# One fused kernel of block-causal attention and two feed-forward layers: the first pair's queries and keys are issued from ScalarE's queue, and a table shifts the order of the later instructions

## The chip, the cores and the metric

The kernel runs on one core of a Trainium2 chip. The metric is the device time of one execution in microseconds, as the median of several runs; lower is better. A profiled execution has a span, which is the time from its first to its last instruction, and a device time of its own, which is a little longer.

Five engines work side by side, each with a fixed sequence of instructions: TensorE (PE for its matmuls, PEld for its weight loads), VectorE (DVE), ScalarE (ACT), GpSimd (POOL) and SyncE (SP, which here only issues DMAs). An engine waits on semaphores for the others and never overtakes within its own sequence.

## What is computed

The reference, cut to what matters:

```python
def _attn_ref(q, k, v):                       # 4 batches, 8 heads, 576 positions, head size 64
    scores = scale * np.matmul(q, k.transpose(0, 1, 3, 2))
    mask = block_i >= block_j                 # blocks of 64 positions
    scores = np.where(mask, scores, -1000000000.0)
    attn = np.exp(scores - np.max(scores, axis=-1, keepdims=True))
    attn = attn / (np.sum(attn, axis=-1, keepdims=True) + 1e-09)
    return np.matmul(attn, v)

x = attn_out.transpose(0, 2, 1, 3).reshape(2304, 512)
h = np.maximum(np.maximum(x @ w1, x @ w2), x @ w3)      # 512 -> 768
x = h @ w_out                                           # 768 -> 512
h = np.maximum(x @ w_in, 0.0)                           # 512 -> 2048
out = h * h @ w_out2                                    # 2048 -> 512
```

The weights arrive as 64-bit floats and are turned into 32-bit ones on the chip.

## The kernel before

**Stages.** Heads are taken in pairs: pairs 0 to 3 are batch 0, pairs 4 to 7 batch 1, and so on to pair 15. `attn_pair` computes a pair in steps of 128 query rows: scores on TensorE (tiles `sc`, `sc_t`), the mask and the row maximum on VectorE (`nm`), the exponential with its row sum on ScalarE (`P`, `sm`), transposes on TensorE (`tp`), copies of these (`ta`, `tb`), and the product with the values (`av`). For batch 0 the queries and keys of a first group of 256 positions go as plain floats straight from a DMA into the scores; `score_operands_f32` issues the three DMAs of a pair into one tile, `zk0` for pair 0 and `zk1` for pair 1, and `zk_early` for pairs 2 and 3. `mlp1` is the first feed-forward layer on a block of tokens (tiles `l`, `run`, `hh`, `hl`, then `ys`); `mlp1(0)` needs only batch 0's first group, so its matmuls stand beside the attention of the rest. It multiplies in two parts: each 32-bit weight chunk is split in a high and a low part (`w1h`, `w1l` for the first matrix, `wo` for the second). `load_w_` brings one chunk of 128x512 weights: one DMA of 512 KB, two activations on ScalarE, two operations on VectorE, one addition on GpSimd, then a copy on ScalarE for the high part and a subtraction on VectorE for the low part. There are 18 chunks of the first matrices and 6 of `wo`. While attention runs, `quad_forms` prepares the weights of the second feed-forward layer and stores them (`wst` to `ws_d`). From about 364 us on TensorE has only `mlp1` and then the second layer (`ph_x`, `ph_z`, `acc_x`, `acc_z`, `acc_y`) to do.

**The order of the work is made by a planner.** All calls go through the class `Plan`. `note` records an operation with its number, its rank and what it depends on, and `issue` then plays the whole list against a small model of durations and semaphore delays: whichever engine can start something earliest takes, of the operations that can start then, the one with the lowest rank, and among these the lowest number. The operations are issued in that order, so that each engine's sequence is fixed when the program is built. Attention has rank 0, `mlp1` rank 1 (so that its matmuls fill what attention leaves), evictions of `mlp1` rank -1, and the preparation of the second layer's weights rank 2. An operation marked for `nc.any` goes to ScalarE or VectorE, whichever comes first in the model. `issue` runs twice: once for everything up to `mlp1(3)` and `quad_forms`, and once for the rest. Because every instruction goes through `call`, the profile gives most of them one line, L190, and they are told apart by their tiles.

**The start.** A table load and an activation of one column make ScalarE ready for the exponential (L374). GpSimd builds a 128x128 identity. TensorE multiplies that identity with itself eight times (tile `idle`, 16 instructions). SyncE issues the first weight chunk (`raw_w`), then the three DMAs of `zk0`, the values of pair 0, a second weight chunk, the three of `zk1`, and so on.

Of the kernel before, what the change touches and what calls it, by code (L numbers as in the profile page):

```python
# [12 lines left out]
F32 = mybir.dt.float32  # L13
# [135 lines left out]


class Op:
    def __init__(self, index, engines, name, args, kw, rank):
        self.index, self.engines, self.name, self.args, self.kw, self.rank = index, engines, name, args, kw, rank
        self.deps, self.after, self.makes = set(), [], []
        self.engine = self.end = None
# [16 lines left out]
class Plan:  # L172
    def __init__(self, tc):
        self.tc, self.ops, self.rank = tc, [], 0
        nc = tc.nc
        self.real = dict(pe=nc.tensor, dve=nc.vector, act=nc.scalar, pool=nc.gpsimd, sp=nc.sync)
        self.free = dict(pe=1450.0, dve=900.0, act=2240.0, pool=1300.0, sp=740.0)
        self.held, self.queue = dict(dve=0.0, pool=0.0), 0.0
        self.tensor, self.vector, self.scalar = [Engine(self, (e,)) for e in ("pe", "dve", "act")]
        self.gpsimd, self.sync, self.any = [Engine(self, e) for e in (("pool",), ("sp",), ("act", "dve"))]  # L180
# [47 lines left out]

    def issue(self):

        ops, free, held, queue = self.ops, self.free, self.held, self.queue
        left = [0 for op in ops]
        users = [[] for _ in ops]
# [18 lines left out]
        for _ in ops:  # L252
            best = None
            for e, w in waiting.items():
                if not w:
                    continue
                other = held["pool" if e == "dve" else "dve"] if e in held else 0.0
                start = {i: max(free[e], at, other if port else 0.0) for i, (at, port) in w.items()}
                t = min(start.values())
                i = min((i for i, s in start.items() if s <= t), key=lambda i: (ops[i].rank, i))  # L260
                if best is None or t < best[0]:
                    best = t, e, i
# [27 lines left out]
class Engine:  # L290
# [3 lines left out]
    def __getattr__(self, name):  # L294
        return lambda *args, **kw: self.plan.note(self.engines, name, args, kw)


HOLD = dict(dve=120, pool=60)
# [63 lines left out]
def fused_kernel(ctx: ExitStack, tc: tile.TileContext, z0, k0, kz0, qk, v, w123, wo1, win2, wo2, out):  # L362
# [8 lines left out]

    warm = const.tile([128, 1], F32, name="warm")
    tc.nc.vector.memset(warm, 0.0)
    tc.nc.scalar.activation(out=warm, in_=warm, func=AF.Exp)  # L374
    make_identity(tc.nc, ident.tile.real)
    dram = Pool(nc, dram)
# [9 lines left out]
    def bank(name, tag):  # L386
        return ps.tile([128, 512], F32, tag=tag, bufs=BANKS[tag], name=name)


    idle = bank("idle", "av")  # L390
# [108 lines left out]
    def score_operands_f32(n, g):  # L499


        if g == 0:
            if n < 2:
                zk = at.tile([128, 3, GA], F32, tag="tb", bufs=2 * CFG["TB"][1], name=f"zk{n}")
            else:
                if not early:
                    early.append(m1.tile([128, 8, 3, GA], F32, tag="wo1", name="zk_early"))
                zk = early[0][:, n]
# [43 lines left out]
    def attn_pair(n, groups=(0, 1)):  # L552
# [27 lines left out]
        def step(i):  # L580
# [13 lines left out]
            for h in range(2):  # L594
                for c, (qp, kp) in enumerate(score[h]):
                    mm(sc[h][:, :N], qp[:, 128 * i - q0:128 * i - q0 + 128], kp[:, :N], start=c == 0,
                       stop=c == len(score[h]) - 1)
                if not share:
                    nc.vector.memset(sc[h][0:64, N - 64:N], MASKED / scale)
                    nc.vector.tensor_reduce(out=nm[:, h:h + 1], in_=sc[h][:, :N], axis=AX.X, op=ALU.max, negate=True)  # L600
# [256 lines left out]
    with nc.behind(marks[CFG["WO"]][0]), nc.ranked(2):  # L857
        for q in range(NQ):
            quad_forms(1, q)
        for q in range(EARLY):  # L860
            quad_forms(0, q)
    nc.issue()
    es_a.close()
# [312 lines left out]
```

## Time and profile before

| what | value |
|---|---|
| median of three runs | 838.93 us (838.79 to 840.89) |
| the profiled execution | 840.18 us |
| its span, first to last instruction | 838.4 us |
| TensorE busy with matmuls | 825.8 us (99%) |
| TensorE idle in the span | 12.6 us |
| VectorE busy, ScalarE busy | 625.0 us (75%), 474.4 us (57%) |

Times below are microseconds from the span's start. An engine's busy share is an average over stages that are bound by different things, so it has to be read stage by stage. A matmul's end is modelled in the profile and matmuls overlap, so a short wait between two of them need not show as idle time.

### The profile page before, as it was taken

The numbers are of one execution on the slowest core, as the hardware profiler recorded it, in microseconds if no ns is written. First come the engines' busy times: TensorE is split into PE (matmuls) and PEld (weight loads), VectorE is DVE, ScalarE is ACT, GpSimd is POOL, SyncE is SP. The second block draws the span as 40 slices with busy tenths as digits, with TensorE's granted clock in tenths as the row PEclk, the third lists the DMA queues.
The fourth block names the chain that finished last, engine by engine and source line by source line (L and its number), as shares of the span: only waits on it lengthen the run. The fifth ranks groups of instructions, "written<-read, shape, count | busy, mean of one in ns | idle before, by whom it ended". The sixth has DMA issues, their size and how long they took to land.

```text
span 838.4 us, 14621 instructions
## 1 busy us (share of the span) xinstructions
PE 825.8 (99%) x5008; PEld 779.2 (93%) x5008; DVE 625.0 (75%) x1347; ACT 474.4 (57%) x1099; POOL 108.0 (13%) x98
## 2 busy tenths in 40 slices
PE   8999999999999999999999999999999999999998
PEld 6678899988999889999999999999999999999998
DVE  7989789888889988817877557987269855478562
ACT  7999678788778767736554224544124552233441
POOL 2343111221122212202221000000000000000000
PEclk9999999999999999999999999999999999999999
DMA  9755455665566656254796867888988889988882
GB/s 326 263 162 171 124 175 182 203 224 183 167 206 206 199 192 201 77 194 150 264 352 228 312 203 248 286 292 271 306 257 255 257 249 288 293 256 254 246 272 85
DMA packets 92203, 190.24 MB, mean 227 GB/s; under 512 B 9697, under 2 KB 18913, under 8 KB 92129
## 3 DMA queue, kind: packets, MB, share of 16 engines
q1 hardware_dynamic: 92128, 189.31, 69.2%
q8 instruction: 40, 0.66, 0.3%
q14 instruction: 35, 0.28, 0.1%
HBM read 150.47 MB, written 38.80 MB: 226 GB/s over the span
## 4 chain that ended last, share of the span: by engine, by line
PE 90%; DVE 5%; ACT 3%; DMA 1%; POOL 1%; issue 1%; POOLq 0%; ACTq 0%; DVEq 0%
PE l L190 33%; PE ph_x L190 12%; PE acc_x L190 12%; PE ph_z L190 9%; PE acc_z L190 6%; PE av L190 4%; PE sc L190 4%; PE tp L190 3%; PE acc_y L190 3%; PE sc_t L190 2%; DVE nm L190 1%; DMA raw_w<-in_wo 1%; PE tp_t L190 1%; DVE w1l L190 1%; ACT P L190 1%
## 5 line engine op out<-in xcount | busy, mean ns | idle before, releaser
L190 PE MATMUL l<-xhl,w1h 128*128 128x432 f32 (+2 forms) x864 | 230.6, 344 | 0.5 <-DVE xhl L190 0.5
L190 PEld LDWEIGHTS l<-xhl,w1h 128*128 128x128 f32 x864 | 154.0, 188 | 7.5 <-DVE xhl L190 1.2
L190 PE MATMUL l<-xhl,w1l 128*128 128x432 f32 (+2 forms) x432 | 149.7, 347 | 0.6 <-DVE run L190 0.5
L190 PEld LDWEIGHTS l<-xhl,w1l 128*128 128x128 f32 x432 | 81.3, 188 | 5.8 <-DVE run L190 1.4
L190 PE MATMUL ph_x<-t,ws 128*128 128x384 f32 x432 | 80.9, 335 | 0.0
L190 PE MATMUL l<-hh,wo 128*128 128x432 f32 (+2 forms) x288 | 77.5, 344 | 1.2 <-DVE wo L190 1.1
L190 PEld LDWEIGHTS ph_x<-t,ws 128*128 128x128 f32 x432 | 75.6, 188 | 0.0
L190 ACT ACTIVATE P<-sc,nm 128x128 f32<-128x128 f32 (+3 forms) x128 | 67.3, 535 | 11.5 <-DVE nm L190 10.0
L190 DVE TENSOR_TENSOR run<-l,run 128x432 f32<-128x432 f32 (+2 forms) x72 | 39.8, 553 | 32.6 <-PE l L190 29.4
L190 POOL TENSOR_TENSOR f_w<-f_w,raw_w 128x512 int32<-128x512 int32 x30 | 41.5, 1384 | 148.2 <-DVE f_w L190 33.4
L190 DVE TENSOR_REDUCE nm<-sc 128x2 f32<-128x256 f32 (+2 forms) x96 | 55.0, 590 | 0.8
L190 PEld LDWEIGHTS l<-hh,wo 128*128 128x128 f32 x288 | 51.9, 188 | 3.7 <-DVE wo L190 1.3
L190 PE MATMUL acc_x<-g_p,ws 128*128 128x384 f32 x288 | 54.0, 335 | 0.0
L190 PE MATMUL ph_z<-b,ws 128*128 128x384 f32 x288 | 53.9, 335 | 0.0
L190 PE MATMUL tp<-ident,P 128*128 128x128 f32 x320 | 49.9, 275 | 1.1 <-ACT rs L190 0.5
L190 PEld LDWEIGHTS acc_x<-g_p,ws 128*128 128x128 f32 x288 | 50.5, 188 | 0.0
L190 PEld LDWEIGHTS ph_z<-b,ws 128*128 128x128 f32 x288 | 50.4, 188 | 0.0
L190 PE MATMUL l<-hl,wo 128*128 128x432 f32 (+2 forms) x144 | 49.2, 342 | 0.0
L190 PEld LDWEIGHTS tp<-ident,P 128*128 128x128 f32 x320 | 38.8, 141 | 8.9 <-ACT P L190 1.3
L190 PE MATMUL av<-tb,v 128*64 128x320 f32 (+1 forms) x256 | 42.9, 410 | 0.0
L190 ACT COPY tb<-tp 128x384 f32<-128x384 f32 (+1 forms) x64 | 32.4, 539 | 13.4 <-PE tp L190 12.9
L190 DVE TENSOR_TENSOR g_p<-c_wo,g_p 128x768 fp32r<-128x768 f32 x24 | 22.9, 956 | 16.8 <-ACT g_p L190 16.8
(188 smaller groups left out, 1746.5 us busy)
## 6 DMA issues: line engine op xcount, KB each, us to landing
ws<-ws_d SPq DMA_DIRECT2D x336, 256.0 KB, 4.0
ws_d<-wst SPq DMA_DIRECT2D x70, 256.0 KB, 4.4
raw<-in_qk SPq DMA_DIRECT2D x24, 576.0 KB, 4.3
ws_d<-wst SPq DMA_DIRECT2D x21, 512.0 KB, 7.1
raw_w<-in_w SPq DMA_DIRECT2D x18, 512.0 KB, 4.8
raw_w<-in_wo SPq DMA_DIRECT2D x16, 512.0 KB, 4.3
raw_wi<-in_win SPq DMA_DIRECT2D x14, 512.0 KB, 5.8
v<-in_v SPq DMA_DIRECT2D x16, 320.0 KB, 3.8
```

Of the source, the lines that this page charges most:

```text
L190: return getattr(engine, op_name)(*map(value, args), **{k: value(x) for k, x in kw.items()})
```

## The change

The three DMAs of pair 0's first group leave the planner's list. They are issued from ScalarE's own queue, first queries, keys, second queries, before ScalarE's table load; the code of the table load and of the identity moves behind them. SyncE's queue goes on as before without these three. The planner's model is told of it by three landing times (`landing`), a later start of ScalarE and a later first transfer. A constraint of order is added between the two heads' matmuls of a step that share a bank. And the table `MOVES` gives 342 operations, named by their number, a shift of rank and a shift of number; the first call of `issue` chooses by the shifted pair (`place`). Numbers count the operations in the order in which the code notes them, without the three DMAs that left the list. The second call of `issue` has no table.

```diff
+MOVES = (
+    (267, 0, -2893), (290, -0.5, -738), (344, 0, 679), (378, 0, 485), (380, 0.5, 609), (384, -5.5, 1226), (399,
...
+    4695), (501, 3.5, 3242), (508, 5, 1439), (552, -0.5, 1882), (573, 11.5, -8305), (580, 6.5, -379), (582, -2,
...
+    (3756, 10.5, -4016), (3797, 14.5, -1676),
+)
...
 class Op:
     def __init__(self, index, engines, name, args, kw, rank):
         self.index, self.engines, self.name, self.args, self.kw, self.rank = index, engines, name, args, kw, rank
+        self.place = rank, index
...
-        self.free = dict(pe=1450.0, dve=900.0, act=2240.0, pool=1300.0, sp=740.0)
-        self.held, self.queue = dict(dve=0.0, pool=0.0), 0.0
+        self.free = dict(pe=1450.0, dve=900.0, act=2240.0 + 1290.0 * FIRST, pool=1300.0, sp=740.0)
+        self.held, self.queue = dict(dve=0.0, pool=0.0), 2440.0 + 1020.0 * FIRST
...
+    def landing(self, view, when):
+
+        op = Op(-1, ("sp",), "dma_start", (), dict(out=view), 0)
+        op.engine, op.end = "sp", when
+        view.tile.first = view.tile.first or op
+        view.tile.writes.append((op, view.area))
+        view.tile.users.append(op)
+
-    def issue(self):
+    def issue(self, moves=()):
 
         ops, free, held, queue = self.ops, self.free, self.held, self.queue
+        for i, rank, place in moves:
+            ops[i].place = ops[i].rank + rank, ops[i].index + place
...
-                i = min((i for i, s in start.items() if s <= t), key=lambda i: (ops[i].rank, i))
+                i = min((i for i, s in start.items() if s <= t), key=lambda i: ops[i].place)
...
+FIRST = 1
...
-    warm = const.tile([128, 1], F32, name="warm")
-    tc.nc.vector.memset(warm, 0.0)
-    tc.nc.scalar.activation(out=warm, in_=warm, func=AF.Exp)
-    make_identity(tc.nc, ident.tile.real)
...
+    zk_first = []
+    for n in range(FIRST):
+        zk = at.tile([128, 3, GA], F32, tag="tb", bufs=2 * CFG["TB"][1], name=f"zk{n}")
+        zk.tile.make()
+        for i, (h, src) in enumerate(((0, z0[n, :, 0:GA]), (2, k0[n, :, :GA]), (1, z0[n, :, GA:2 * GA]))):
+            nc.landing(zk[:, h], 3400.0 + 380.0 * (3 * n + i))
+            tc.keep_in_program_order(tc.nc.scalar.dma_start(out=zk.tile.real[:, h], in_=src))
+        zk_first.append(zk)
+    warm = const.tile([128, 1], F32, name="warm")
+    tc.nc.vector.memset(warm, 0.0)
+    tc.keep_in_program_order(tc.nc.scalar.activation(out=warm, in_=warm, func=AF.Exp))
+    make_identity(tc.nc, ident.tile.real)
...
         if g == 0:
+            if n < FIRST:
+                return [[(zk_first[n][:, h], zk_first[n][:, 2])] for h in range(2)], None
...
-                    mm(sc[h][:, :N], qp[:, 128 * i - q0:128 * i - q0 + 128], kp[:, :N], start=c == 0,
-                       stop=c == len(score[h]) - 1)
+                    op = mm(sc[h][:, :N], qp[:, 128 * i - q0:128 * i - q0 + 128], kp[:, :N], start=c == 0,
+                            stop=c == len(score[h]) - 1)
+                    if share and h and c == 0:
+                        op.after.append(first)
+                    first = op
...
-    nc.issue()
+    nc.issue(MOVES)
     es_a.close()
```

Read against the code, the table's entries fall on 161 operations of TensorE, 96 of VectorE, 73 of ScalarE and 12 that either of the last two may take. Of TensorE's, 57 are matmuls of `mlp1`, of which 44 get a higher rank (later) and 13 a lower one; 104 are matmuls or transposes of attention, of which 80 get a lower rank (earlier) and 24 a higher one. The lowest number, 267, is the copy that makes the high part of the eighth weight chunk. 573 is the subtraction that makes the low part of the second `wo` chunk, 580 and 639 are the copies that make the high parts of the third and the sixth.

## Rows read from the trace of the kernel before

**Rows 1.** The page: busy time, share of the span, instructions; then the chain.

```profile
PE 825.8 (99%) x5008; PEld 779.2 (93%) x5008; DVE 625.0 (75%) x1347; ACT 474.4 (57%) x1099; POOL 108.0 (13%) x98
...
PE 90%; DVE 5%; ACT 3%; DMA 1%; POOL 1%; issue 1%; POOLq 0%; ACTq 0%; DVEq 0%
```

**Rows 2.** Windows: length, busy time (instructions) by engine, granted TensorE clock, DMA share, GB/s.

```profile
0.00:7.00 7.00, 5.51 (x24) 5.04 (x24) 1.20 (x4) 2.72 (x4) 1.30 (x7) 1.00 0.71 235
7.00:28.00 21.00, 17.36 (x116) 11.25 (x114) 20.78 (x61) 18.88 (x59) 7.57 (x6) 1.00 1.01 369
28.00:97.00 69.00, 66.54 (x510) 54.11 (x508) 61.04 (x151) 61.31 (x150) 25.36 (x19) 1.00 0.53 166
97.00:364.00 267.00, 265.64 (x1732) 243.28 (x1732) 229.14 (x654) 203.11 (x569) 54.51 (x54) 1.00 0.56 183
364.00:484.00 120.00, 120.00 (x619) 115.07 (x614) 79.47 (x140) 55.12 (x101) 19.27 (x14) 1.00 0.71 253
484.00:838.40 354.40, 350.80 (x2020) 350.44 (x2018) 233.41 (x339) 133.28 (x217) 0.00 (x0) 1.00 0.81 255
```

**Rows 3.** Waits of PE, whole span: engine tile <- releaser: total us, times, longest.

```profile
PE sc L190 <- DMA zk<-in_k: 1.4, 1, 1.4
PE idle L190 <- POOL ident masks.py:199: 1.4, 1, 1.4
PE l L190 <- DVE wo L190: 1.1, 1, 1.1
...
PE tp_t L190 <- DVE P_t L190: 0.6, 1, 0.6
```

**Rows 4.** Timeline 0 to 9.7: start, duration, engine, operation; idle before and its releaser.

```profile
0.73 1.28 ACT L374 ACT_TABLE_LOAD   x1 [0.73 <-PEq L1169]
0.74 0.38 SPq L190 DMA_DIRECT2D raw_w<-in_w  x1
...
1.17 0.42 SPq L190 DMA_DIRECT2D zk<-in_z  x1
...
1.36 3.78 PE L190 MATMUL idle<-ident 128*128 128x128 f32 x16 [1.36 <-POOL ident masks.py:199]
1.64 0.42 SPq L190 DMA_DIRECT2D zk<-in_k  x1
2.02 0.20 ACT L374 ACTIVATE warm<-warm 128x1 f32<-128x1 f32 x1
...
4.40 1.24 ACT L190 ACTIVATE raw_w<-raw_w 128x512 f32<-128x512 f32 x2 [2.18 <-DMA raw_w<-in_w]
...
5.24 1.67 PEld L190 LDWEIGHTS sc<-zk 128*128 128x128 f32 x8 [0.40 <-issue]
...
5.56 0.69 DVE L190 SCALAR_TENSOR_TENSOR raw_w<-raw_w 128x512 int32<-128x512 int32 x1
...
6.98 0.17 DVE L190 MEMSET sc<- 64x128 f32 x1 [0.72 <-PE sc L190]
...
8.74 1.55 PE L190 MATMUL sc<-zk 128*128 128x128 f32 x8 [1.42 <-DMA zk<-in_k]
```

**Rows 5.** DMA, 0 to 8 us: GB/s by slices of 0.2 us; issues and landing.

```profile
GB/s 0 0 0 0 0 0 0 0 61 164 20 82 143 328 307 512 389 374 338 369 374 364 292 200 220 246 348 400 420 415 374 379 451 338 307 313 369 364 389 359
...
zk<-in_z SPq DMA_DIRECT2D x4, 128.0 KB, 4.3
```

**Rows 6.** Timeline 93.5 to 96.3, around the last `wo` chunk.

```profile
93.50 1.31 POOL L190 TENSOR_TENSOR f_wo<-f_wo,raw_wo 128x512 int32<-128x512 int32 x1 [6.28 <-DVE f_wo L190]
...
94.84 0.62 ACT L190 CAST wo<-f_wo 128x512 fp32r<-128x512 f32 x1 [0.70 <-POOL f_wo L190]
...
95.49 0.69 DVE L190 TENSOR_TENSOR wo<-f_wo,wo 128x512 fp32r<-128x512 f32 x1 [0.17 <-ACT wo L190]
```

**Rows 7.** Timeline of PE, 155 to 157 us.

```profile
155.26 0.31 PE L190 MATMUL l<-xhl,w1l 128*128 128x320 f32 x1
155.41 0.46 PE L190 MATMUL l<-xhl,w1h 128*128 128x320 f32 x2
155.71 0.31 PE L190 MATMUL l<-xhl,w1l 128*128 128x320 f32 x1
156.59 0.63 PE L190 MATMUL tp_t<-ident,P_t 128*128 128x128 f32 x4 [0.58 <-DVE P_t L190]
```

58 rows, old and new, of the table MOVES are left out of this document.

## The prediction

> **What bounds the kernel now.** I read the page first: TensorE's matmuls are busy 99% of the span and hold 90% of the chain of waits, VectorE 5%, ScalarE 3% [rows 1]. So a change of order can give back at most the time in which TensorE stands still, and the second question is where that time lies. The windows answer it [rows 2]; the idle time of a stage is its length less its busy PE:
>
> - 0 to 7 us: 7.00 - 5.51 = 1.49, nearly all of it the wait for the identity, 1.4 [rows 3]
> - 7 to 28: 21.00 - 17.36 = 3.64
> - 28 to 97: 69.00 - 66.54 = 2.46
> - 97 to 364: 267.00 - 265.64 = 1.36
> - 364 to 484: none
> - 484 to the end: 354.40 - 350.80 = 3.60
>
> The sum is 12.55. The last 3.60 lie in the part that the second call of the planner orders, without the table, and from 364 us TensorE is full, so whatever TensorE saves before 364 shows one for one at the end. In 7 to 28 VectorE is busy 20.78 of 21.00 us and the DMA engines are full: there TensorE waits because others have no time left. In 28 to 97 VectorE and ScalarE are at 61 of 69, and TensorE's longest wait is for the last `wo` chunk, 1.1 [rows 3], behind GpSimd, ScalarE and VectorE in a row [rows 6].
>
> These idle times are a little too small, because a matmul's modelled end hides part of a wait. In [rows 7] three matmuls of 320 columns start within 0.45 us (155.26 to 155.71), 0.15 each; the one of 155.71 should have been followed at 155.86, and the transposes start at 156.59. That is 0.73 lost, where the row says 0.58, a factor of 1.26.
>
> **The change, part by part.**
>
> *Three DMAs leave SyncE's queue.* SyncE issues one per 0.47 us (1.17 to 1.64, [rows 4]), so each later issue of SyncE can be 3 x 0.47 = 1.41 us earlier: the values of pair 0, the second weight chunk, `zk1`, and all behind them. But the DMA engines move over 300 GB/s from 2.6 us on, and from 1.6 to 2.6 only 61, 164, 20, 82 and 143, in the mean 94 [rows 5]. At the 369 that they hold later [rows 2], the second queue can bring forward (369 - 94) x 1.0 us, 0.28 MB, or 0.75 us of transfers; the other half of the 1.41 us is only a longer queue of requests.
>
> *ScalarE issues three DMAs.* At SyncE's pace that is 1.41 us, from 0.73 to 2.14; the table load (1.28) and the warming activation (0.20) follow and end at 3.62. What hides it is the wait for the first weight chunk, which ends at 4.40 [rows 4]: 0.78 us of cover. Queued behind it on ScalarE is only that chunk; without the cover VectorE's two operations on it, GpSimd's addition and the first low part come later.
>
> The Trainium skill (page "ScalarE: Activation LUTs", section "What ACT_TABLE_LOAD costs") speaks against this part: it gives the load 1283 ns and a drain of some 1380 ns behind it. The load here does take 1.28 us, but the next activation starts at 2.02, when 0.73 + 1.28 = 2.01, so no drain stands behind it [rows 4]. By the page ScalarE would be ready at 5.0 instead of 3.6, some 0.6 after the chunk's 4.40, and by the row it costs nothing; I go by the row.
>
> *`zk0` lands earlier.* Issued at 0.73, 1.20 and 1.67 instead of 1.17 and on, it gains 0.44 at each. What then stops pair 0's scores is TensorE itself: the 16 identity instructions run from 1.36 for 3.78 us, to 5.14, and the scores' weight loads start at 5.24 after 0.40 of idle [rows 4]. So the first scores gain 0.40 at most. Against it: `zk0` now runs beside the first weight chunk. If all its 384 KB came before the chunk's last bytes, the chunk would land 0.39 MB / 369 GB/s = 1.07 us later, at about 5.5; VectorE's two operations on it, which end at 5.56 + 0.69 = 6.25, would end near 7.3, past the mask of the first scores at 6.98 [rows 4], and from there VectorE is full: a loss of some 0.3, up to 0.6 if the scores are early. I take a gain of 0.3, since the scores head the chain and the chunk's work has 0.7 us of slack before 6.98.
>
> *`zk1` lands earlier.* TensorE waits 1.42 us for it [rows 4]. With 0.75 us of transfers gained about half of that wait would go. But the work behind it is VectorE's (mask, maximum), which has 0.22 us to spare in the 21 us from 7 on [rows 2]: TensorE would wait for VectorE a little later instead. I count nothing, and 1.4 as the upper bound.
>
> *The added constraint of order* adds no instruction and no semaphore; the first of two heads' matmuls already came first. Nothing.
>
> *The table.* It adds and removes no operation; only waits can change. Its lowest number is the copy of the eighth weight chunk, so most of what happens before 28 us keeps its rule and moves only with the start. Within reach are the idle times of 28 to 97 and 97 to 364: 2.46 + 1.36 = 3.82, or with the factor of [rows 7] 3.82 x 1.26 = 4.8 us. The pattern of the entries, `mlp1` matmuls later and attention's earlier, keeps filler for the times when attention waits, which is what those stages lack. Against it: the stages are short of VectorE and ScalarE too, 96 and 73 operations of which are also moved, and the waits left are each of 0.2 to 1.1 us, about the size of what a planner's model of semaphores and DMA landings misses. Between 0 and 4.8 I take the half, 2.4. On the other side, new waits: entries 573, 580 and 639 put three operations of `wo` chunks far back. A chunk's last pass, GpSimd to VectorE, is 93.50 to 95.49 + 0.69 = 96.18, 2.7 us [rows 6]; one or two chunks late by so much cost 2.7 to 5.4.
>
> *Sum.* Against the profiled execution of 840.18 us: -0.3 for the start, -2.4 for the table, 837.5. The median of the runs is 1.25 below that execution, so in the runs' terms 838.93 - 2.7 = 836.2 us.
>
> **Rivals.**
>
> 1. *The start gains, the table only moves waits about.* The stages from 28 to 97 are nearly full on three engines, so a wait removed at one place comes back at another. Then 838.93 - 0.3 = 838.6. For it: VectorE and ScalarE at 88% [rows 2]. Against it: from 97 to 364 both have room (229 and 203 of 267).
> 2. *The order works as a whole.* All of 4.8, 0.4 at the start and 1.4 at `zk1`: 838.93 - 6.6 = 832.3. For it: TensorE's waits are few and single, most of them once in the span [rows 3]. Against it: full VectorE before 28.
> 3. *Slower: a `wo` chunk comes late.* `mlp1(0)`'s second half and every later block need all of `wo`; TensorE already stands still for it for 1.1 us [rows 3], and there attention of batch 1 is just beginning and gives it little else. With one chunk 2.7 late and nothing won elsewhere: 838.93 - 0.3 + 2.7 = 841.3; with two, 844.0. It decides when the new wait is longer than what the table wins elsewhere, that is from 2.4 + 0.3 us on. For it: the entries with +11.5 and +6.5. Against it: an operation put back still starts whenever its engine has nothing else ready in the model.
> 4. *The head start does nothing or harms,* since the chunk and `zk0` share the DMA engines: 0 to +0.6 in place of -0.3, and with the table 836.5 to 837.1. The Trainium skill says so of the bandwidth ("DMA: Bandwidth & Descriptors", section "Issuing engines are not separate DMA queues"): the queues interleave on the same 16 engines, and a second one only saves the time of issuing. No row of before has two queues at once; by that rule 836.5.
>
> **How the numbers follow.** A change under 0.3%, 2.5 us here, can't be told from none. My forecast with rival 4 has a chance of 0.45; its own range, with 1.2 us either way on the table, is 835.0 to 837.5 and straddles the bound of 836.4, so I put 0.31 of it with faster and 0.14 with same. Rival 1 has 0.27, all same. Rival 2 has 0.15, faster. Rival 3 has 0.13, slower; of it the lighter half lies below 841.4 and I leave it with slower all the same, as entries not looked at can add to it. Faster 0.46, same 0.41, slower 0.13. The range takes in rival 1 and most of the way to rival 2, and up to one `wo` chunk partly late: 832.8 to 840.6.
>
> **What would show it.** The first weight load of `sc` from `zk` at about 4.9 instead of 5.24, the table load at 2.1 and ScalarE's first chunk still near 4.4; a start past 5.0 for that chunk is rival 4. PE busy in 7 to 28 about as before. Idle PE of 28 to 97 and 97 to 364 falling from 3.8 together to about 1.9: at 3.8 it is rival 1, near 0 rival 2. The wait of `l` for `wo` stays under 1.1; at 2.5 or more it is rival 3. From 364 us on the span has the same length, 474.4 us of it. The prediction is wrong if PE's busy time itself changes, for instance because matmuls alternate more often between kinds and run less densely, which the idle time doesn't show.

## The result, and the profile after

The changed kernel is slower: a median of 848.36 us (847.43 to 849.1, four runs) against 839.17 us (838.79 to 840.89, four runs) for the kernel before on the same chip. The ratio is 1.0099, with a 95% interval of 1.008 to 1.0118. That lies above the predicted range (832.8 to 840.6), with the other sign than the forecast. The profiled execution took 848.05 us, with a span of 846.3. The versions below ran on several chips, each beside the kernel before on the same chip, so they are compared by their ratios to it and not by their medians (which here differ by 9.2 us). Ratios are given in points of a per cent: 0.1 point is 0.84 us, and the change costs 0.99 points, 8.3 us.

The page of the changed kernel: busy time, share and instructions by engine, then the granted TensorE clock in 40 slices.

```profile
PE 832.5 (98%) x5008; PEld 781.1 (92%) x5008; DVE 628.4 (74%) x1349; ACT 474.7 (56%) x1097; POOL 106.6 (13%) x98
...
PEclk9899999999999999999999999999999999999999
```

TensorE has the same 5008 matmuls as in [rows 1] and is busy 832.5 - 825.8 = 6.7 us longer with them. The span grew by 7.9, so idle time accounts for only 1.2 of it. And the clock, 1.00 in every window of [rows 2], shows an 8 in one slice near the start. The windows of the changed kernel, with the columns of [rows 2]:

```profile
0.00:7.00 7.00, 4.89 (x20) 4.23 (x20) 0.06 (x1) 2.69 (x4) 0.70 (x6) 1.00 0.73 258
7.00:28.00 21.00, 16.05 (x101) 11.21 (x103) 19.31 (x60) 17.50 (x52) 7.16 (x5) 0.88 0.97 334
28.00:97.00 69.00, 68.43 (x499) 54.68 (x496) 61.41 (x147) 61.96 (x155) 26.59 (x19) 0.96 0.53 174
97.00:364.00 267.00, 264.59 (x1712) 238.60 (x1712) 231.38 (x653) 201.45 (x565) 52.17 (x53) 1.00 0.55 178
364.00:484.00 120.00, 120.00 (x627) 114.48 (x626) 82.30 (x151) 56.61 (x107) 20.02 (x15) 1.00 0.72 256
484.00:846.30 362.30, 358.56 (x2059) 357.86 (x2057) 233.94 (x340) 134.45 (x219) 0.00 (x0) 1.00 0.80 252
```

Three things are to be seen. The windows up to 28 us hold 121 matmul records, before 140; those up to 364 us hold 2332, before 2382: the loss arises in two portions, early and spread over the attention. From 28 to 97 the idle time is 69.00 - 68.43 = 0.57 instead of 2.46, in part because matmuls stay busy longer at the clock of 0.96; from 97 to 364 it is 2.41 instead of 1.36. What of this is the table's is seen only beside the new plan without it (Round 1). And in 7 to 28 VectorE is busy 19.31 instead of 20.78, GpSimd and ScalarE less too: nobody is full there any more, everything waits in turn.

The waits of PE over the whole span (columns of [rows 3]):

```profile
PE r L256 <- DVE sm L256: 1.8, 1, 1.8
PE tp L256 <- ACT P L256: 1.6, 2, 1.1
...
PE sc L256 <- DMA zk<-in_z: 1.2, 1, 1.2
...
PE l L256 <- DVE wo L256: 0.4, 1, 0.4
```

The wait for the last `wo` chunk fell from 1.1 to 0.4. In its place stand two new ones: 1.2 for the second queries of pair 0, and 1.8 for row sums that VectorE delivers late.

The timeline of the changed kernel, first 0 to 12, then the two engines from 24 to 28:

```profile
0.73 0.41 ACTq L470 DMA_DIRECT2D zk<-in_z  x1
...
1.65 0.45 ACTq L470 DMA_DIRECT2D zk<-in_z  x1
...
2.13 1.28 ACT L474 ACT_TABLE_LOAD   x1 [2.13 <-issue]
...
4.71 1.21 ACT L256 ACTIVATE raw_w<-raw_w 128x512 f32<-128x512 f32 x2 [1.07 <-DMA raw_w<-in_w]
...
5.59 1.11 PE L256 MATMUL sc<-zk 128*128 128x128 f32 x4 [0.45 <-DMA zk<-in_k]
...
7.91 0.92 PE L256 MATMUL sc<-zk 128*128 128x128 f32 x4 [1.20 <-DMA zk<-in_z]
...
8.49 0.17 DVE L256 MEMSET sc<- 64x128 f32 x1 [7.63 <-PE sc L256]
...
24.84 0.87 PE L256 MATMUL av<-ta,v 128*64 128x256 f32 x8
27.52 0.87 PE L256 MATMUL r<-ident,sm 128*64 128x128 f32 x5 [1.81 <-DVE sm L256]
...
25.80 1.28 DVE L256 TENSOR_TENSOR w1l<-f_w,w1h 128x512 fp32r<-128x512 f32 x2
27.00 0.15 DVE L256 TENSOR_SCALAR sm<-sm 128x4 f32<-128x4 f32 x1
```

The second queries are issued at 1.65, about when the keys ahead of them were issued before [rows 4], so one place earlier, and the matmuls that need them still start only at 7.91. The first mask is at 8.49 instead of 6.98. At 25.80 two subtractions of weight chunks stand in VectorE's sequence ahead of the small row-sum operation of 27.00 that TensorE waits for.

Around these standstills TensorE runs at half clock: from 9.5 us, after a wait of 1.20 and during one of 1.15, and from 26.5, before the wait that ends at 27.52 is over. Windows of the changed kernel, chosen around the two stretches:

```profile
9.40:12.90 3.50, 2.92 (x10) 2.49 (x11) 3.45 (x8) 3.43 (x12) 1.28 (x1) 0.51 0.91 324
...
25.40:27.40 2.00, 0.31 (x6) 0.07 (x2) 2.00 (x9) 2.00 (x5) 0.05 (x1) 0.78 0.93 243
26.50:33.40 6.90, 5.88 (x23) 4.27 (x24) 4.75 (x16) 5.51 (x19) 2.77 (x2) 0.51 0.43 140
```

A granted clock of 0.51 is, but for the windows' edges, the lower of the two levels, 1.2 GHz; in the same two stretches the kernel before ran 20 and 48 matmuls at 1.00.

And one tile is denser in one kernel than in the other. The windows of the whole span for the tile `av` alone, last line (sum of busy time by engine), first the kernel before, then the changed one:

```profile
sum 838.40, PE 49.57 PEld 37.24 DVE 5.18 ACT 11.22; mean PE 16.52 PEld 12.41 DVE 1.73 ACT 3.74
```

```profile
sum 846.30, PE 53.28 PEld 36.17 DVE 5.24 ACT 11.05; mean PE 17.76 PEld 12.06 DVE 1.75 ACT 3.68
```

The products with the values are the same matmuls in both, and they take 53.28 - 49.57 = 3.71 us longer. Busy times of tiles overlap, so they don't add up to TensorE's; but the rest of the 6.7 us goes with the half clock, as two versions below show (row sums first, small operations early). Their `av` sum is the same 53.28, their profiled clock is 1.00 throughout, and TensorE is busy 829.8 and 829.4 us, 4.0 and 3.6 above the kernel before.

### The profile page after: what moved, and what is told of

The parts are those of the page before. It is cut to its first block, busy times and chain, and to the rows that moved or that the text cites. A ratio compares the mean times of both kernels' runs of the same rounds, so it can differ in the third digit from the quotient of the medians.

```text
span 846.3 us, 14572 instructions
## 1 busy us (share of the span) xinstructions
PE 832.5 (98%) x5008; PEld 781.1 (92%) x5008; DVE 628.4 (74%) x1349; ACT 474.7 (56%) x1097; POOL 106.6 (13%) x98
## 4 chain that ended last, share of the span: by engine, by line
PE 89%; DVE 7%; DMA 2%; issue 1%; ACT 0%; SPq 0%; DVEq 0%; ACTq 0%
PE l L256 31%; PE ph_x L256 12%; PE acc_x L256 12%; PE ph_z L256 9%; PE acc_z L256 6%; PE av L256 5%; PE sc L256 4%; PE tp L256 4%; PE acc_y L256 3%; DVE nm L256 2%; PE sc_t L256 1%; DMA raw<-in_qk 1%; PE tp_t L256 1%; DVE P L256 1%; DVE f_w L256 1%
## 5 line engine op out<-in xcount | busy, mean ns | idle before, releaser
L256 PE MATMUL l<-xhl,w1h 128*128 128x432 f32 (+2 forms) x864 | 228.1, 344 | 0.4 <-DVE xhl L256 0.4
L256 DVE TENSOR_TENSOR run<-l,run 128x432 f32<-128x432 f32 (+2 forms) x72 | 39.8, 553 | 33.4 <-PE l L256 31.8
L256 DVE TENSOR_REDUCE nm<-sc 128x1 f32<-128x384 f32 (+2 forms) x96 | 55.1, 592 | 1.0
L256 DVE TENSOR_SCALAR P<-P,sm 128x128 f32<-128x128 f32 (+3 forms) x96 | 38.5, 435 | 0.8
```

Of the source, the lines that this page charges most:

```text
L256: return getattr(engine, op_name)(*map(value, args), **{k: value(x) for k, x in kw.items()})
```

## The experiments

Four questions: is it the start, the new order, the table, or how the matmuls follow each other? Unless a diff says otherwise an edit leaves the rest of its kernel as it is, and all kernels do the same arithmetic.

### Round 1: the two halves of the change

**Order of before, new start.** The planner's order stays; only the three DMAs of `zk0` go out on ScalarE's queue ahead of the table load.

```diff
+    for h, src in ((0, z0[0, :, 0:GA]), (2, k0[0, :, :GA]), (1, z0[0, :, GA:2 * GA])):
+        tc.keep_in_program_order(tc.nc.scalar.dma_start(out=zk_first.tile.real[:, h], in_=src))
     warm = const.tile([128, 1], F32, name="warm")
```

> The order of before on every engine, planned as before; only the three DMAs of zk0 are moved, to ScalarE's queue ahead of the table load. The changed kernel is 9.2 us slower than before. Theory 'start and order': the head start itself does harm (the second queue's 1 KB packets lose against SyncE's 4 KB packets, the second head's queries come at 7.9 instead of 5.8 us, TensorE stands still and its granted clock falls), and the new order adds to it: 842 to 845 us. Rival 'order alone': the start is harmless, 839 +- 1. Rival 'start alone': 847 to 849, all of the loss.

841.39 us, ratio 1.0012 (1.0002 to 1.0023): about 1.0 us slower. The head start gives nothing and costs a little, by itself.

**Order of after, old start.** The order that the changed kernel's planner makes, with the three DMAs on SyncE's queue behind the first weight chunk.

```diff
-            tc.keep_in_program_order(tc.nc.scalar.dma_start(out=zk.tile.real[:, h], in_=src))
+            nc.deferred.append(lambda zk=zk, h=h, src=src: tc.keep_in_program_order(
+                tc.nc.sync.dma_start(out=zk.tile.real[:, h], in_=src)))
```

> The order of the changed kernel, table and all, but zk0's three DMAs are issued by SyncE behind the first weight chunk, as before. 'Start and order': 841 to 845 us. 'Order alone': 847 to 849. 'Start alone': 838 to 840; the table would then be worth nothing or a little.

846.1 us, ratio 1.0076 (1.0061 to 1.0091). 0.76 of the 0.99 points are in the order of the instructions; the interval overlaps that of the changed kernel, so the other 0.23, the start's, are not clear of noise.

**New start, no table.**

```diff
-    nc.issue(MOVES)
+    nc.issue()
```

> The changed kernel with an empty table: the planner knows of the new start and orders by rank and number alone. If the table is the harmful part of the order: 840 to 844 us. If the table is worth what I forecast (2.4) and the loss is the start's: 850 to 852. If the table changes nothing: 847 to 849.

850.22 us, ratio 1.0113 (1.0088 to 1.0138). Without the table it is no better (the intervals overlap): the order is bad before the table touches it. What the planner is told of the new start makes another plan. Two things that it is told count for nothing: played without ScalarE's later start, or without the added constraint of order, its code puts the operations of every engine in the same order. What is left is the landing times, the first transfer 1.02 us later and the three DMAs that are off its list. Two windows of this kernel:

```profile
28.00:97.00 69.00, 66.40 (x486) 53.76 (x486) 58.31 (x148) 63.42 (x160) 25.37 (x18) 0.98 0.49 163
97.00:364.00 267.00, 262.72 (x1702) 238.49 (x1702) 227.46 (x650) 200.05 (x557) 55.87 (x56) 0.99 0.56 184
```

Its idle times there are 2.60 and 4.28. Against these, the changed kernel's 0.57 and 2.41 show the table removing idle time in both.

**Queues swapped.** To see why `zk0` comes late on ScalarE's queue, the queues change places: SyncE begins with `zk0`, ScalarE's queue brings the first weight chunk.

```diff
+            if e == "sp" and self.lead:
+                real, self.lead = self.real["act"], False
...
-            tc.keep_in_program_order(tc.nc.scalar.dma_start(out=zk.tile.real[:, h], in_=src))
+            tc.keep_in_program_order(tc.nc.sync.dma_start(out=zk.tile.real[:, h], in_=src))
```

> The order of the changed kernel; SyncE's queue begins with zk0's three DMAs (1 KB packets) and ScalarE's queue brings the first weight chunk (4 KB packets) ahead of the table load. Theory 'packets in turn': where two queues stand on the same DMA engines a packet is taken from each in turn, whatever its size, so 128 packets of the chunk pass beside 128 of zk0's 384 and zk0 then has the engines alone: the chunk's activation starts at 4.0 to 4.4, the first scores at about 5.0 and the second head's without a wait, and the time falls by 2 to 6 us against the changed kernel. Rival 'ScalarE's queue is slow by itself': the chunk comes past 5.5 us and zk0 by 4.5.

847.07 us, ratio 1.0087 (1.0072 to 1.0103), 0.12 points below the changed kernel, with overlapping intervals: the 2 to 6 us that were expected aren't there. The second queries no longer come late, since the first eight matmuls start together:

```profile
5.38 1.97 PE L257 MATMUL sc<-zk 128*128 128x128 f32 x8 [0.24 <-DMA zk<-in_k]
```

So TensorE's wait for them is not what makes most of the loss. The DMA view from 0 to 9 us tells the two causes apart. First the changed kernel's queues (packets, MB, share) and issues (KB, median us to landing), then those of this one:

```profile
q1 hardware_dynamic: 1101, 2.08, 66.6%
q10 hardware_dynamic: 432, 0.39, 13.1%
...
zk<-in_z ACTq DMA_DIRECT2D x2, 128.0 KB, 5.2
```

```profile
q1 hardware_dynamic: 1383, 1.94, 64.9%
q10 hardware_dynamic: 144, 0.52, 16.1%
...
raw_w<-in_w ACTq DMA_DIRECT2D x1, 512.0 KB, 4.1
zk<-in_z SPq DMA_DIRECT2D x4, 128.0 KB, 4.1
```

`zk0` goes in packets of about 0.39 MB / 432 = 0.9 KB, a weight chunk in packets of about 0.52 MB / 144 = 3.6 KB. With `zk0` on ScalarE's queue (q10) its DMAs take 5.2 us to land, where [rows 5] has 4.3. The packet records give, from 2.5 to 3.5 us, 30 KB per half microsecond on q10 beside 135 to 143 KB on q1. Swapped, from 2.5 to 3.0, q10 carries the big packets and moves 102 KB while q1 moves 37. So ScalarE's queue isn't slow; the queue with the small packets gets the small share of the bytes, as if the two were served packet by packet: in these half microseconds of the changed kernel, 29 and 31 packets on q10 stand beside 35 and 33 on q1. The Trainium skill ("DMA: Bandwidth & Descriptors", section "Queues, rings and completion order") says that each DMA engine takes turns between its queues at packet granularity; these counts agree, as far as the trace's packets are the page's.

### Round 2: one wait, or the heads' turns

Two theories for the order: the standstill at 25.4 with the half clock behind it, or the density of the `av` matmuls. In these kernels the planner's choices are first gathered in a list, which is rearranged and then issued.

**Row sums first** (order of after, old start). Two small VectorE operations of pair 2 are moved ahead of pair 3's second row maximum, so that TensorE doesn't stand still for them.

```diff
+    sums = [x for x in order if written(x[1]) == "sm2_0" and x[0] == "dve"]
+        at = next(i for i, (e, op) in enumerate(order) if e == "dve" and written(op) == "nm3_1")
+        order[at:at] = sums
```

> The kernel with the new order and the old start (5.7 us slower than before), with two VectorE operations moved ahead: the addition and the reciprocal of pair 2's row sums (sm) now stand before the row maximum of pair 3's second step, not behind two low-part subtractions. Nothing else moves. In that kernel TensorE waits 1.6 us for them at 24 to 25.7 us and its granted clock then reads 0.5 for 6.8 us. Theory 'one wait and the clock': both go, the time falls by 3 to 4 us. Rival 'the wait only moves', since VectorE is full there: it falls by less than 1 and the clock falls elsewhere.

845.98 us, ratio 1.0077 (1.0059 to 1.0095), against 1.0076 without the edit: nothing gained. Waits of PE, and the stretch around the old standstill:

```profile
PE tp L257 <- ACT P L257: 4.2, 3, 2.5
```

```profile
25.40:27.40 2.00, 0.42 (x2) 0.23 (x3) 2.00 (x8) 0.95 (x5) 0.00 (x0) 1.00 0.88 356
```

The wait for `sm` is gone and the clock stays at 1.00 in this profile (two of the four executions have 0.998), but TensorE now waits 2.5 us at the same place for ScalarE's `P`: VectorE's operations had only changed places, and pair 3's maximum was late instead. The theory that this one wait and the clock behind it make the loss, which expected 3 to 4 us, falls.

**Heads in turn** (order of after, old start). All products of a step's accumulator are issued where its last one stood, in the order in which the code notes them, which alternates between the two heads.

```diff
+def heads_in_turn(order):
+    groups = {}
+    for x in order:
+        if x[0] == "pe" and re.match(r"av\d", written(x[1])):
+            groups.setdefault(written(x[1]), []).append(x)
+    for group in groups.values():
+        at = order.index(group[-1])
+        order = [x for x in order[:at] if x not in group] + sorted(group, key=lambda x: x[1].index) + order[at + 1:]
+    return order
```

> The kernel with the new order and the old start, with the value products (av) of each accumulator gathered at the place of their last one, in the order in which the code notes them, the two heads in turn. The two heads' products write different halves of the columns, and in the trace two that alternate start within 14 ns of each other, where two of the same head are 160 to 270 ns apart. The table's shifts of single av matmuls break the alternation in six blocks (1.9, 0.4, 1.0, 0.7, 0.5 us longer). Theory 'halves in parallel': the time falls by 2 to 4.5 us. Rival 'filler': the other matmuls that stand between have their place, and it falls by less than 1.

841.67 us, ratio 1.0027 (1.0015 to 1.0039): 0.49 points, 4.1 us, come back by this alone.

**Both edits.**

```diff
+        order = sums_early(order)
+        order = heads_in_turn(order)
```

> Both edits on the kernel with the new order and the old start. If they are the two causes of the order's 5.7 us and are independent, the time falls by 5 to 8 us and stands at 0.993 to 1.001 of the kernel before; if one of the theories fails, by 2 to 4.

842.68 us, ratio 1.0031 (1.0017 to 1.0046): like heads in turn alone.

**Heads in turn in the kernel before.**

```diff
+        order = heads_in_turn(order)
+        for e, op in order:
```

> The kernel before, with only the value products put in turn as above. Its own twelve blocks of 28 products take 3.01 us each, and the blocks of the changed kernel in which the heads alternate throughout take 2.85. 'Halves in parallel' expects 12 x 0.16 = 1.9 us less than before (a ratio of 0.998). Rival: no change, if the 3.01 us hide a wait of something else.

837.63 us, ratio 0.998 (0.9969 to 0.999): 1.9 us faster than the kernel before, and the fastest version here. The timeline of PE shows why. First the changed kernel, one block of products (the two heads' matmuls have the same line and tile):

```profile
184.98 1.56 PE L256 MATMUL av<-tb,v 128*64 128x320 f32 x5
186.11 0.43 PE L256 MATMUL av<-ta,v 128*64 128x256 f32 x1
```

then the same block with heads in turn:

```profile
181.48 0.87 PE L190 MATMUL av<-ta,v 128*64 128x256 f32 x8
182.18 2.11 PE L190 MATMUL av<-tb,v 128*64 128x320 f32 x16
184.12 0.28 PE L190 MATMUL av<-t,v 128*64 128x64 f32 x4
```

In the first, five products of one head and one shape start one by one within 186.11 - 184.98 = 1.13 us, 0.28 from each to the next; in the second, sixteen products of both heads start within 184.12 - 182.18 = 1.94 us, 0.12 each. Each writes 64 of TensorE's 128 columns, the two heads different halves. In the records of the second block two neighbours of different heads start 6 or 7 ns apart, and the next pair of this shape 262 ns later; in the first, neighbours of the same head start about 270 ns apart. The chains give this block's length (start, duration, what), in the kernel before, after, and with heads in turn:

```profile
182.12 3.01 PE av L190 x23
```

```profile
185.05 3.98 PE av L256 x22
```

```profile
181.55 2.85 PE av L190 x28
```

(The trace has all 28 products of each block; the chain counts those that lie on it.) The tile's busy sum falls to about 47.7 in the kernels with the heads in turn (the misfit table of Round 4 apart), here the kernel before with the edit:

```profile
sum 835.60, PE 47.69 PEld 29.55 DVE 5.19 ACT 11.21; mean PE 15.90 PEld 9.85 DVE 1.73 ACT 3.74
```

49.57 - 47.69 = 1.88 us, which is what the run gained. The Trainium skill ("TensorE: Matmul & The Clock Gate", section "The mechanism" of its part on packing small matmuls) has matmuls at different positions of the array overlap with starts some 4 ns apart; here it is 6 or 7, and the turns decide whether there is such a neighbour.

### Round 3: the rest, and the start again

**One DMA for `zk0`** (order of before, heads in turn). The host lays the first pair's queries and keys side by side, so that one DMA with rows of 3 KB on ScalarE's queue replaces three.

```diff
+    tc.keep_in_program_order(tc.nc.scalar.dma_start(out=zk_first.tile.real.rearrange("p h n -> p (h n)"), in_=zk0))
```

> The order of before with the heads in turn (0.998 of before), and zk0 from ScalarE's queue ahead of the table load as in the change, but as one DMA with rows of 3 KB in place of three with rows of 1 KB (the host lays pair 0's queries and keys side by side). 'Packets in turn': its 128 packets pass beside 128 of 4 KB, the first scores start at 5.0 to 5.3 us without a wait for the second head, and the time is 0.3 to 1.0 us below that of the same kernel with the old start, 0.997 of before. If the second queue is slow whatever its packets: 1 us above it, 0.999.

838.53 us, ratio 0.9983 (0.9974 to 0.9993): the same as without it (0.998). The second head no longer waits for its queries, which fits the turns by packet. But both ends of the start come later than from SyncE's queue:

```profile
5.53 1.24 ACT L191 ACTIVATE raw_w<-raw_w 128x512 f32<-128x512 f32 x2 [2.86 <-DMA raw_w<-in_w]
...
5.78 1.58 PE L191 MATMUL sc<-zk 128*128 128x128 f32 x8 [0.68 <-DMA zk<-in_zk]
```

The chunk's activation stood at 4.40 and the scores' first weight load at 5.24 [rows 4].

**Small operations early** (order of after, old start). Beside the two row-sum operations, the two scalings of pair 3's maxima go right behind the maximum of pair 3's second step, so that none of them stands behind the weight chunks. (The expectation counts six operations; the edit's condition picks these four.)

```diff
+        small = [x for x in order if x[0] == "dve" and (written(x[1]) == "sm2_0" or
+                 written(x[1]) in ("nm3_0", "nm3_1") and x[1].name == "tensor_scalar")]
```

> New order, old start, with six small VectorE operations moved right behind the row maximum of pair 3's second step: the two on pair 2's row sums (as in the run with these alone, where TensorE's wait only moved to the next operation in VectorE's sequence, pair 3's scaled maximum) and the scalings of pair 3's maxima. The two low-part subtractions that the new order puts ahead of them now stand behind. Theory 'two weight subtractions ahead of attention': TensorE's standstill at 23 to 28 us goes and the time falls by 2 to 3.5 us against the kernel with the new order and the old start, to a ratio of 1.003 to 1.005. Rival 'VectorE is full, something else waits': it falls by less than 1.

846.44 us, ratio 1.0078 (1.0059 to 1.0096): again nothing, with a clock of 1.00 throughout the profile. TensorE now waits elsewhere:

```profile
PE tp L257 <- ACT P L257: 3.0, 3, 1.3
PE sc L257 <- DMA zk_early<-in_k: 1.9, 2, 1.4
```

**Both of these** (small operations early, heads in turn; order of after, old start).

```diff
+        order = small_early(order)
+        order = heads_in_turn(order)
```

> The same with the heads' value products in turn. If the new order's loss is these two things, a ratio of 0.998 to 1.0005 to the kernel before; if the standstill only moves, 1.002 to 1.003 as with the heads alone.

840.78 us, ratio 1.0014 (1.0004 to 1.0024). 0.64 points below it without heads in turn; beside heads in turn alone (1.0027) the intervals overlap, so what the small operations give isn't shown.

**The same in the changed kernel,** with its start.

> The changed kernel itself, new start and all, with both repairs of the order. The new start costs 1.0 us in the order of before and 2.3 in the new order, so it should stand 1 to 2.5 us above the run with the same repairs and the old start. If the new start's harm is what the bad order makes of it, the two are within 0.5.

842.12 us, ratio 1.003 (1.0019 to 1.0041): 0.16 points more than with the old start, with intervals that just overlap.

### Round 4: plan, table and heads apart

**The plan made anew, alone** (no table, old start).

```diff
-    nc.issue(MOVES)
+    nc.issue()
```

> Old start and no table, but the order that the planner makes when it is told of the new start (ScalarE free 1.3 us later, zk0 landing at 3.4 to 4.2, the first transfer behind it). On the chip nothing differs from before except the order. Theory 'the plan made anew is the larger part': 1.007 to 1.010 of before, since the same order with the new start stands at 1.0113. Rival 'the table's entries make the loss': 0.999 to 1.002.

849.13 us, ratio 1.0114 (1.0095 to 1.0133). The largest single loss, 9.6 us, and neither table nor start is in it. Its waits of PE and its window of 97 to 364:

```profile
PE l L257 <- DVE wo L257: 2.5, 2, 1.4
PE r L257 <- DVE sm L257: 1.8, 1, 1.8
```

```profile
97.00:364.00 267.00, 262.73 (x1703) 239.31 (x1700) 229.16 (x657) 202.77 (x566) 55.12 (x55) 1.00 0.55 183
```

The late row sums are there, so are late `wo` chunks (2.5), and the idle time of that window is 4.27 instead of 1.36. The table (1.0114 to 1.0076) gains 0.38 points, 3.2 us, on this plan.

**Heads in turn in the changed kernel,** nothing else.

```diff
+        order = heads_in_turn(order)
```

> The changed kernel, new start, plan and table, with only the heads' value products in turn. With the old start this was worth 4 us; if it is the same here, 1.0045 to 1.006 of before. If the new start's standstills hide it, over 1.008.

842.95 us, ratio 1.0034 (1.0023 to 1.0044): 0.65 points, 5.5 us, less than the changed kernel. The tile's sum:

```profile
sum 839.60, PE 47.67 PEld 29.72 DVE 5.24 ACT 11.17; mean PE 15.89 PEld 9.91 DVE 1.75 ACT 3.72
```

53.28 - 47.67 = 5.61, about what the run gained. TensorE's whole busy time falls further, by 832.5 - 824.3 = 8.2 us, with a profiled clock of 0.999 instead of 0.994, and its idle time rises by 1.5.

**The table on the plan of before** (old start, old start values, entries renumbered by the three DMAs that stayed in the list, heads in turn).

```diff
-    nc.issue()
+    nc.issue([(i + 3, rank, place) for i, rank, place in MOVES])
```

> Old start, planned as before, with the table (numbers raised by 3, so that they name the same operations) and the heads' value products in turn. The order up to some 30 us is that of before, since the table names nothing earlier. If the early plan was the loss and the table's shifts of everything else are worth something by themselves: 0.993 to 0.997 of before, below the order of before with the heads in turn (0.998). If the table only fits the plan that it was made on: 0.999 to 1.004.

885.26 us, ratio 1.0536 (1.0509 to 1.0564). Waits of PE:

```profile
PE sc L256 <- ACT P L256: 10.2, 10, 2.2
```

**The table without its entries for `av` matmuls** (changed kernel).

```diff
-    nc.issue(MOVES)
+    nc.issue([m for m in MOVES if not (nc.ops[m[0]].name == "matmul" and nc.ops[m[0]].args[0].tile.kw["name"].startswith("av"))])
```

> The changed kernel with the entries of the table left out that name a value product; everything else, the other entries among it, is as in the change. If these entries alone break the heads' turns: 1.004 to 1.006 of before. If other entries or the plan break them too, over 1.008.

878.87 us, ratio 1.0461 (1.0444 to 1.0477). These last two are misses as repairs, and say the same: the table is made for one plan. A shift means something only beside the choices around it; with another plan, or a part of the table, the same numbers cost 39 to 45 us against the kernel before. The longest waits are between scores and exponentials (10.2 and 8.2 us); TensorE is also busy 18.5 and 21.9 us longer than before, at a mean clock of 0.984 and 0.982, so the waits alone are not the whole cost.

## Why the prediction was wrong

**The step that failed most: "most of what happens before 28 us keeps its rule and moves only with the start".** The rule stayed, the start values of the model didn't. The text ahead of the prediction lists the three landing times, ScalarE's later start and the later first transfer as parts of the change; the prediction gave what they do to the plan no term. They (ScalarE's later start apart) make another plan from the first operations on: the small row sums behind weight chunks at 25.80, late `wo` chunks. Alone this costs 9.6 us. Which wait of it costs how much isn't settled: repairing the most visible one, twice, gave nothing, since the next one stood behind it.

**"It adds and removes no operation; only waits can change."** The second failure. 6.7 of 7.9 us of added span are busy time: some 3.7 are the `av` tile, whose heads in turn bring 4.1 to 5.5 us back, and some 3 go with the half clock. A shift of single operations breaks the alternation of two heads. The prediction's last sentence named just this (matmuls that alternate otherwise run less densely, unseen by the idle time) and gave it no rival and no price. The kernel before already lost a little by it, 3.01 us instead of 2.85 for a block of 28, which only the later runs show.

**The table's term, -2.4.** Against the kernel before, the idle time of 28 to 97 fell further than the half that was taken (2.46 to 0.57) and that of 97 to 364 rose (1.36 to 2.41); against the new plan without the table both fell (2.60 and 4.28). Its net gain on the new plan is 3.2 us with the old start (1.0114 to 1.0076), and 1.2 with the new one (1.0113 to 1.0099), where the intervals overlap. So sign and size were about right, partly by luck, against the wrong base: the plan that it was weighed on was not the plan that it acts on. Of its work it gives back some 3.2 us in the heads' turns (the tile's sum is 50.11 us with the new plan and no table, 53.28 with it).

**The start's term, -0.3.** Wrong in sign: 1.0 slower with the old order, 1.9 with the new (1.0076 to 1.0099), 1.3 with both repairs (1.0014 to 1.003), none without the table (1.0114 and 1.0113). Each of these differences but the first is between two ratios and carries some 0.15 to 0.3 points of uncertainty, 1.3 to 2.6 us, so only the first and, barely, the third are clear of zero. Rival 4 had the place, the shared DMA engines, and 0 to +0.6. What it missed is who loses: it priced the chunk as the late one (1.07 us), while it is `zk0` itself, in small packets, whose second queries come at 7.9. ScalarE's chunk went from 4.40 to 4.71 only. That these late queries are the start's cost isn't shown: with the queues swapped they come in time, and the ratio is not shown to fall. The table load cost nothing, as said: activation at 3.43, right behind 2.13 + 1.28. One reading of the term was off: [rows 5] has 292, 200, 220 and 246 GB/s from 4.4 to 5.2 us, not over 300 throughout; nothing hangs on it here.

**Rival 3, a late `wo` chunk,** is in the new plan without the table (2.5 in two waits, the longer 1.4) and not in the changed kernel (0.4): with the table that wait is gone, not made. Which entries do it was not tried.

**The sum of what the runs show:** +9.6 for the new plan, -3.2 for the table, +1.9 for the start, 8.3, the measured loss. The terms are successive steps from one kernel to the next, so they add up by construction; that each step would cost the same in another order is not shown, and the 1.9 for the start lies within its uncertainty.

**Open.** The new order with the old start, heads in turn and small operations early is still 1.2 us above the kernel before, and 2.9 above that kernel with its heads in turn (1.0014 against 0.998); where that arises isn't settled. The half clock of 9.4 to 12.9 and 26.5 to 33.4 goes with standstills. In the profiles of two versions it is gone and the ratio stayed, but a new wait came in each. That it costs something by itself is suggested by executions of one kernel, which differ in their mean clock: the new start without the table took 847.71 us at 1.000, 849.10 at 0.998, 851.35 at 0.992 and 851.54 at 0.991, and with both repairs and the old start seven executions at 1.000 took 839.81 to 841.22 and three at 0.997 or 0.998 took 841.85 to 841.95. The changed kernel's four don't fall into this order. But the main loss isn't the clock's: at 1.000, the new start without the table is still 7.3 us above the median of the kernel before on its chip (840.37).

## What to carry to other kernels

A planner's start values are part of its program: a model told of other landing times and a first transfer 1 us later makes a different plan everywhere behind it, so cost the plan made anew by itself, and a hand-made or searched table of shifts only on the exact plan that it was made for. Look at busy time by tile and not only at waits: the matmuls here that write half of the columns want a neighbour on the other half, and a busy TensorE hides when they have none. Before a transfer is moved to a second queue to come earlier, compare the row sizes of what runs beside it.

## What the runs showed of the hardware

- Matmuls of 64 columns by two heads in different halves, 320 elements each: 6 or 7 ns between the starts of a pair when the heads alternate, about 270 when the same head follows itself; 2.85 us for a block of 28 with the heads in turn, 3.98 in the longest such block of the changed kernel.
- Two DMA queues at once: the one with rows of 1 KB moved 30 to 37 KB per half microsecond beside 102 to 143 KB on the one with rows of about 4 KB, whichever engine issued it (2.5 to 3.5 us of the changed kernel, 2.5 to 3.0 with the queues swapped).
- The granted clock fell to 0.5 at 9.5 us, after a wait of TensorE of 1.20 us and within one of 1.15, and at 26.5, within the wait of 1.81 that ended at 27.5, and stayed there for 3.4 and 6.8 us; the kernel before ran at 1.00 throughout.
